# Routing, diagonals, scatters and row loads moved in a three-stage fused kernel, and one matmul group moved in each of its steps

## The chip, the cores and the metric

The kernel runs on one core of one Trainium2 chip. A core has five engines, each with an instruction queue of its own: TensorE (PE in the profile; its weight loads are PEld), VectorE (DVE), ScalarE (ACT), GpSimd (POOL) and SyncE (SP, which here only issues DMAs). They meet through semaphores. The metric is device time in microseconds (us); lower is better.

## The reference

Three layers follow each other on 3072 tokens (4 batches of 768), each of 384 values (8 heads of 48). The first is a recurrence over time, the second sends each token to one of 8 experts, the third is a dense layer.

```python
for t in range(S):                                   # 4 batches, 8 heads, 768 steps, 48 x 48 states
    cur = np.einsum('bhd,bhe->bhde', u[None] * kt, vt)
    y[:, :, t] = np.einsum('bhd,bhde->bhe', rt, state + cur)
    state = w[None, :, :, None] * state + np.einsum('bhd,bhe->bhde', kt, vt)
...
expert_idx = np.argmax(x @ w_gate, axis=1)           # one of 8 experts for each token
for e in range(E):
    xe = x[expert_idx == e]
    out[expert_idx == e] = gate_w[expert_idx == e, None] * (np.maximum(xe @ w1[e], 0.0) @ w2[e])
...
h = x @ w_in                                         # 384 -> 2048 -> 384
return (np.maximum(0.01 * h, h) @ w_out)
```

## The kernel before

**Attention: 24 units, 25 steps.** The recurrence is cut into units of one batch and 128 time steps; unit `n` is batch `n % 4`, chunk `n // 4`. The loop `for n in range(NU + 1)` in `attention` issues one step for each unit, pipelined by hand: nothing is scheduled later, every engine runs its instructions in the order of this text. In step `n`, PE does `scores(n)` (`pa`), then for unit `n-1` `values` (`py`: first the product of the state `St` with `R`, then that of `A` with `v`) and `update` (`pu`), then `rows(n-2)` (`pr`). DVE masks the scores into `A`, makes `K` and `R` two units ahead, reduces `av`, and adds `pu` to the state. ACT makes the diagonal of `A` (`prep_diag`, eight instructions), copies `py` to `xT`, decays `St`, and copies the rows out. POOL makes `rk` (two instructions) three units ahead and `kr`. `py`, `pa` and `pu` have one buffer each.

**Routing and scatter.** Four units (one chunk of all batches) are a group. `ROUTE_AT` says in which step each of the four parts of a group's routing is issued; they give the expert of each token and `ix`, its row in `xs` in DRAM. `SCATTER_AT` says in which step each unit's 128 rows are scattered there: an indirect DMA that POOL issues (`xs<-rows,ix`). Behind the scatters of groups 0 to 3, in step 21, POOL issues `load_rows(0)`: the first 256 rows of the expert that leads at half time (`choose_first`, `early_flag`). Some rows of `xs` are zeroed first (`ZERO_AT`, `xs<-z`), and a list of tokens is filled (`none`).

**Experts.** `experts` runs nine windows of rows (`WINDOWS`: two for the first expert, one for each of the others; their sizes are `CAPS`), of eight `f` each. A window's rows are loaded by `load_rows` (tile `erows`, one buffer, `w` partitions of `nj` rows each), turned by PE (`turn`, tile `pt`) into `xe`, and multiplied by PE (`first`: `ph`; `second`: `y`). An expert's weights come in eight pieces (`raw<-in_wE`, three buffers), which ACT (`piece_high`) and DVE or POOL (`piece_low`) split into two parts. All these loads but two are issued by SP, in the order of the text. Beside them the weights of the last layer are converted (`raw<-in_w2nd`, `w2f<-t`).

**The dense layer** (`second_part`, tiles `ph` and `o`) takes the rest of the time, on PE almost without a gap.

Of the kernel before, what the change touches and what calls it, by code (L numbers as in the profile page):

```python
# [36 lines left out]
WARM = 5  # L37
ZERO_AT = 3
# [4 lines left out]
    **{11 + 4 * g + u: [(g, u)] for g in (0, 1) for u in range(4)},  # L43
    19: [(2, 0), (2, 1)],
    20: [(2, 2), (2, 3)],
    21: [(3, u) for u in range(4)],
# [20 lines left out]
CAPS = (480, 456, 432, 416, 400, 392, 384, 372)  # L67
# [17 lines left out]
class Kernel:  # L85
# [150 lines left out]
    def choose_first(self, keep, part):  # L236

        V, G = self.nc.vector, self.nc.gpsimd
        if part == 0:
            f = lambda nm, w=1, dt=F32: keep.tile([1, w], dt, name=nm)  # L240
            _, self.half_key = self.counts(keep, "half", G)
            self.half_mx, self.half_x, self.half_id = f("half_mx"), f("half_x", E), f("half_id")
            self.lead, self.first_i = f("lead", E), f("first_i", 1, I32)
        elif part == 1:
            V.tensor_reduce(out=self.half_mx, in_=self.half_key, axis=AX.X, op=ALU.max)
            G.tensor_scalar(
                out=self.lead, in0=self.half_key, scalar1=self.half_mx, scalar2=None, op0=ALU.is_equal
            )
            G.tensor_tensor(out=self.half_x, in0=self.lead, in1=self.place, op=ALU.mult)
        else:  # L250
            V.tensor_reduce(out=self.half_id, in_=self.half_x, axis=AX.X, op=ALU.add)
            G.tensor_scalar(
                out=self.first_i, in0=self.half_id, scalar1=float(E - 1), scalar2=0.0, op0=ALU.min, op1=ALU.max
            )
# [10 lines left out]
    def early_flag(self, keep, part):  # L265

        V, G = self.nc.vector, self.nc.gpsimd
        if part == 0:
            self.early_cnt, _ = self.counts(keep, "early", G)
            G.tensor_tensor(out=self.early_cnt, in0=self.early_cnt, in1=self.lead, op=ALU.mult)  # L270
# [74 lines left out]
    def attention(self, xs, clist, extra, first_weights, const, route):  # L345
        nc, tc, a = self.nc, self.tc, self.a
        with ExitStack() as ctx:
# [30 lines left out]
            load(1, ("kT", "rT", "k", "r"))  # L378
# [22 lines left out]
            warm, spread = (ps.tile([P, 512], F32, tag="rt", name=nm) for nm in ("warm", "spread"))  # L401
            for i in range(WARM):
                nc.tensor.matmul(warm, self.ident, zeros, start=True, stop=True)
# [60 lines left out]
            def prep_diag(n):  # L464
# [4 lines left out]
                if n >= NU - 2:  # L469

                    flat = d["A"].rearrange("s i p t -> s p i t")
                    nc.gpsimd.tensor_tensor(
                        out=flat, in0=self.ident[:, None, None, :].to_broadcast([P, NP, 2, P]),
                        in1=d["av"].rearrange("s (p i) -> s p i", i=2)[:, :, :, None].to_broadcast([P, NP, 2, P]),
                        op=ALU.mult,
                    )
                    return
# [36 lines left out]

            def values(n):
                d, b, c = st[n], n % B, n // B
                d["py"] = py = ps1.tile([HP, NP, P], F32, tag="py", name="py")
                if c:
                    for p in range(NP):
                        nc.tensor.matmul(  # L520
                            py[:, p, :], St[b][:, p, :], d["R"][:, p, :], start=(p == 0), stop=False,
                            skip_group_check=True,
                        )
                for p in range(NP):
                    for i in range(2):
# [3 lines left out]
                            start=(c == 0 and p == 0), stop=(p == NP - 1), skip_group_check=True,  # L529
# [66 lines left out]
            for n in range(NU + 1):  # L596
# [23 lines left out]
                if 0 <= n - 1 < NU:  # L620
                    values(n - 1)
                    update(n - 1)
                if 0 <= n - 2 < NU - 1:
                    rows(n - 2)
# [15 lines left out]
                if n + 1 < NU - 2:  # L640
                    prep_diag(n + 1)
                prep_av(n + 2)
                if n + 2 >= NU - 2:
                    prep_diag(n + 2)
# [11 lines left out]
                for part, g in ROUTE_AT.get(n, ()):  # L656
# [5 lines left out]
                    self.route(part, g, route, nc.gpsimd if n < 20 else nc.vector, bank)  # L662
# [33 lines left out]
    def route(self, part, g, sm, eng, bank=None):  # L696
# [20 lines left out]
        elif part == 1:  # L717
# [139 lines left out]

    def load_rows(self, i, xs, eng=None):

        k, off, cap = WINDOWS[i]  # L860
        nj = -(-cap // P)
        w = cap // nj
# [6 lines left out]
    def turn(self, i, ps, tag, cs=range(KD)):  # L869
        nc = self.nc  # L870
        k, off, cap = WINDOWS[i]
        nj = -(-cap // P)
        w = cap // nj
# [72 lines left out]
    def experts(self, xs, clist, pools, meanwhile):  # L946
# [361 lines left out]
def main_path(k, ctx, const, out, xs, clist, debug):  # L1308
# [111 lines left out]
```

## Time and profile before

| | before |
|---|---|
| median of 3 runs | 796.58 us (795.02 to 797.38) |
| profiled execution, its own time | 795.89 us |
| its span, first to last instruction | 794.2 us |
| mean granted TensorE clock | 0.977 |
| busy: PE, DVE, ACT, POOL | 755.1, 471.9, 372.5, 198.3 us |
| POOL busy from 81.6 to 131.7 us | 43.79 us |

Busy shares are means over stages. Where two instructions of one engine overlap, a row that merges several counts the time from the first start to the last end.

### The profile page before, as it was taken

The page shows a single profiled execution, that of the slowest core. Times are in us where ns is not written, and L with a number is a line of the kernel's source. Part 1 is how long each engine was busy: PE and PEld are TensorE (multiplying, and loading weights), DVE is VectorE, ACT ScalarE, POOL GpSimd, SP SyncE. Part 2 cuts the span into 40 slices and gives each one's busy share as a digit, 9 for nine tenths or more (in the row PEclk, how much of TensorE's full clock was granted, in tenths as well). Part 3 has the DMA queues.
Part 4 walks back from the last instruction along what each step waited for, and adds up shares of the span by engine and source line. Part 5 has one row for each costly group of instructions (what it writes and reads, how often), then busy time and mean ns, then how long its engine had stood idle before and what let it go on. Part 6 is the DMA issues. An engine that isn't in the chain of part 4 may idle for free.

```text
span 794.2 us, 13196 instructions
## 1 busy us (share of the span) xinstructions
PE 755.1 (95%) x4908; PEld 694.2 (87%) x4908; DVE 471.9 (59%) x837; ACT 372.5 (47%) x785; POOL 198.3 (25%) x216
## 2 busy tenths in 40 slices
PE   6999995989999999799999999999999999999994
PEld 3889884989999999799999899999999999999993
DVE  6898885548888999699873443433333343343330
ACT  6898873355545555356443523332342243233331
POOL 6867885401222222122200110020020001002001
PEclk9999997899999999999999999999999999999997
DMA  8997965368767757757530000010010001001001
GB/s 250 264 272 225 281 223 179 121 184 257 210 193 230 232 183 232 204 162 228 147 111 21 6 35 1 1 40 0 1 40 1 1 0 40 1 1 40 1 1 44
DMA packets 52372, 92.62 MB, mean 117 GB/s; under 512 B 12788, under 2 KB 30761, under 8 KB 52297
## 3 DMA queue, kind: packets, MB, share of 16 engines
q1 hardware_dynamic: 49017, 81.47, 34.6%
q0 software_dynamic: 3280, 10.21, 3.5%
q8 instruction: 40, 0.66, 0.4%
q14 instruction: 35, 0.29, 0.1%
HBM read 73.11 MB, written 18.57 MB: 115 GB/s over the span
## 4 chain that ended last, share of the span: by engine, by line
PE 75%; DMA 9%; POOL 7%; issue 3%; DVE 2%; SPq 2%; ACT 0%; POOLq 0%; ACTq 0%
PE o L1041 25%; PE ph L1022 25%; PE ph L903 12%; PE y L928 11%; DMA r<-in_r 3%; DMA erows<-xs 3%; DMA xs<-z 2%; POOL rk L446 2%; POOL xs L759 2%; POOL rk L447 1%; PE pt L880 1%; DMA raw<-in_wE 1%; SPq L368 1%; POOL kr L451 1%; DMA xs<-rows,ix 1%
## 5 line engine op out<-in xcount | busy, mean ns | idle before, releaser
L1041 PE MATMUL o<-c,gg 128*128 128x384 f32 x1152 | 215.5, 336 | 0.0
L1022 PE MATMUL ph<-x,c 128*128 128x512 f32 x864 | 213.9, 392 | 0.0
L1041 PEld LDWEIGHTS o<-c,gg 128*128 128x128 f32 x1152 | 202.1, 188 | 8.1 <-DVE gg L1031 0.2
L1022 PEld LDWEIGHTS ph<-x,c 128*128 128x128 f32 x864 | 161.2, 188 | 28.5
L1028 DVE TENSOR_TENSOR s<-s,ph 128x512 f32<-128x512 f32 x96 | 65.9, 686 | 165.4 <-ACT s L1027 165.4
L1027 ACT ACTIVATE s<-ph 128x512 f32<-128x512 f32 x96 | 57.4, 598 | 173.9 <-PE ph L1022 162.7
L903 PE MATMUL ph<-xe,c 128*128 128x256 f32 (+8 forms) x648 | 124.8, 338 | 0.0
L928 PE MATMUL y<-hh,c 128*128 128x256 f32 (+8 forms) x648 | 122.4, 333 | 1.2 <-DVE hh L909 0.7
L802 POOL TENSOR_TENSOR c<-raw,c 128x768 fp32r<-128x768 f32 x32 | 60.2, 1880 | 223.3 <-ACT c L794 159.7
L928 PEld LDWEIGHTS y<-hh,c 128*128 128x128 f32 x648 | 110.2, 189 | 3.7 <-DVE hh L909 0.9
L903 PEld LDWEIGHTS ph<-xe,c 128*128 128x128 f32 x648 | 109.8, 192 | 1.9
L1031 DVE TENSOR_TENSOR gg<-s,gg 128x512 fp32r<-128x512 f32 x96 | 66.4, 692 | 67.0 <-ACT gg L1030 66.3
L1054 POOL DMA_INDIRECT out<-z,to x24 | 24.2, 1008 | 320.9 <-ACT z L1053 302.6
L1030 ACT ACTIVATE gg<-s 128x512 fp32r<-128x512 f32 x96 | 60.7, 632 | 81.2 <-DVE s L1028 81.2
L794 ACT ACTIVATE c<-raw 128x768 fp32r<-128x768 f32 x80 | 67.1, 840 | 6.7 <-DMA raw<-in_wE 5.9
L908 ACT ACTIVATE hh<-ph 128x256 fp32r<-128x256 f32 (+8 forms) x72 | 34.4, 478 | 68.5 <-PE ph L903 65.4
L802 DVE TENSOR_TENSOR c<-raw,c 128x768 fp32r<-128x768 f32 x48 | 46.0, 962 | 13.7 <-ACT c L794 12.0
L479 ACT ACTIVATE A<-ident,av 128x128 f32<-128x128 f32 x176 | 53.8, 396 | 0.5 <-DVE av L460 0.4
L849 DVE SCALAR_TENSOR_TENSOR t<-raw,t 128x384 f32<-128x384 uint32 x32 | 44.3, 1384 | 1.1
L909 DVE SCALAR_TENSOR_TENSOR hh<-ph,hh 128x256 fp32r<-128x256 f32 (+8 forms) x72 | 38.5, 535 | 6.1 <-ACT hh L908 5.9
L496 DVE COPY_PREDICATED A<-strict,pa 128x1024 f32<-128x1024 int32 x24 | 32.4, 1351 | 3.1 <-ACT A L479 1.2
L490 PE MATMUL pa<-R,K 48*128 48x128 f32 x384 | 28.2, 287 | 5.8 <-DVE A L496 5.8
(176 smaller groups left out, 681.1 us busy)
## 6 DMA issues: line engine op xcount, KB each, us to landing
raw<-in_wE SPq DMA_DIRECT2D x64, 384.0 KB
raw<-in_w2nd SPq DMA_DIRECT2D x32, 384.0 KB
w2f<-t SPq DMA_DIRECT2D x32, 192.0 KB
raw<-w2f SPq DMA_DIRECT2D x16, 384.0 KB
k<-in_k SPq DMA_DIRECT2D x24, 192.0 KB
r<-in_r SPq DMA_DIRECT2D x24, 192.0 KB
v<-in_v SPq DMA_DIRECT2D x24, 192.0 KB
kT<-in_kT SPq DMA_DIRECT2D x40, 96.0 KB
```

Source lines behind the costliest of these rows:

```text
L479: nc.scalar.activation(out=d["A"][:, h % 2, h // 2, :], in_=self.ident, func=AF.Copy, scale=d["av"][:, h : h + 1],)
L794: self.nc.scalar.activation(out=w[:, 0, c], in_=t, func=AF.Copy)
L802: eng.tensor_tensor(out=w[:, 1, c], in0=t, in1=w[:, 0, c].bitcast(F32), op=ALU.subtract)
L849: nc.vector.scalar_tensor_tensor(out=x, in0=low.bitcast(U32), scalar=2.0**-52, in1=x, op0=ALU.mult, op1=ALU.mult)
L903: nc.tensor.matmul(ph[:, :cap], w[:, wl, c * 512 + o : c * 512 + o + P], self.xT[i][:, xl, c, :cap], start=(c == 0 and n == 0), stop=(c == ...
L928: nc.tensor.matmul(self.y[i][m][:, :cap], w[:, wl, o : o + P], t[:, xl, :cap], start=(f == 0 and n == 0), stop=(f == FF // P - 1 and n == 2),)
L1022: nc.tensor.matmul(ph, w[:, wl, c * 512 + off : c * 512 + off + P], x2[b][:, xl, c, :], start=(c == 0 and i == 0), stop=(c == KD - 1 and i ...
L1027: nc.scalar.activation(out=s, in_=ph, func=AF.Copy, scale=0.01)
L1028: nc.vector.tensor_tensor(out=s, in0=s, in1=ph, op=ALU.max)
L1030: nc.scalar.activation(out=t[:, 0, :], in_=s, func=AF.Copy)
L1031: nc.vector.tensor_tensor(out=t[:, 1, :], in0=s, in1=t[:, 0, :].bitcast(F32), op=ALU.subtract)
L1041: nc.tensor.matmul(o[b][k][:, :DM], t[:, gl, k * P : (k + 1) * P], w[:, wl, (f % 4) * DM : (f % 4 + 1) * DM], start=(f == 0 and i == 0), s ...
```

## The change

Eight edits are made together.

1. In each step PE does the products of `A` with `v` first, then `update`, then those of the state with `R` (now `values_state`). `py` is one tile for the whole loop; the warm-up writes it once.
2. Warm-up matmuls: 3, not 5. The loads of unit 1 are issued with `k` and `r` ahead of `kT` and `rT`. Zeroing and the token list start one step earlier.
3. Scatters of groups 0 and 1 are one step earlier, those of groups 2 and 3 are spread otherwise.
4. `choose_first`, `early_flag` and the one-hot `oh` go from POOL to DVE, and so do the first two parts of group 3's routing (steps 18 and 19).
5. The diagonals of the last two units, on POOL until now, go to ACT like the others.
6. The first expert's weight pieces are split, and pieces 3 to 7 loaded, mostly one step later.
7. `CAPS` are all multiples of 16 (sum 3328, was 3332), and `nj` must divide them: 448 rows are 112 x 4 (was 456, 114 x 4), 400 are 100 x 4 (was 392, 98 x 4), 368 are 92 x 4 (was 372, 124 x 3).
8. From window 2 on, the rows of the next window are issued ahead of the weight piece on SP.

```diff
-WARM = 5
-ZERO_AT = 3
+WARM = 3
+ZERO_AT = 2
 SCATTER_AT = {
-    **{11 + 4 * g + u: [(g, u)] for g in (0, 1) for u in range(4)},
-    19: [(2, 0), (2, 1)],
-    20: [(2, 2), (2, 3)],
-    21: [(3, u) for u in range(4)],
+    **{10 + 4 * g + u: [(g, u)] for g in (0, 1) for u in range(4)},
+    18: [(2, 0)],
+    19: [(2, 1), (2, 2)],
+    20: [(2, 3), (3, 0)],
+    21: [(3, u) for u in range(1, 4)],
     24: [(4, u) for u in range(4)],
 }
...
-CAPS = (480, 456, 432, 416, 400, 392, 384, 372)
+CAPS = (480, 448, 432, 416, 400, 400, 384, 368)
...
     def choose_first(self, keep, part):
-            _, self.half_key = self.counts(keep, "half", G)
+            _, self.half_key = self.counts(keep, "half")
...
     def early_flag(self, keep, part):
-            self.early_cnt, _ = self.counts(keep, "early", G)
+            self.early_cnt, _ = self.counts(keep, "early")
...
-            load(1, ("kT", "rT", "k", "r"))
+            load(1, ("k", "r", "kT", "rT"))
...
+            self.py = ps1.tile([HP, NP, P], F32, tag="py", name="py")
             for i in range(WARM):
-                nc.tensor.matmul(warm, self.ident, zeros, start=True, stop=True)
+                x = self.py.rearrange("q p t -> q (p t)") if i == 1 else warm
+                nc.tensor.matmul(x, self.ident[:, : x.shape[0]], zeros, start=True, stop=True)
...
-                if n >= NU - 2:
-                    flat = d["A"].rearrange("s i p t -> s p i t")
-                    nc.gpsimd.tensor_tensor(
...
+            def values_state(n):
+                d, b = st[n], n % B
+                if n // B:
+                    for p in range(NP):
+                        nc.tensor.matmul(
+                            d["py"][:, p, :], St[b][:, p, :], d["R"][:, p, :], start=False, stop=(p == NP - 1),
+                            skip_group_check=True,
+                        )
...
                     values(n - 1)
                     update(n - 1)
+                    values_state(n - 1)
...
-                    self.route(part, g, route, nc.gpsimd if n < 20 else nc.vector, bank)
+                    self.route(part, g, route, nc.gpsimd if n < 18 else nc.vector, bank)
...
-            if eng is V:
-                V.tensor_tensor(out=d["oh"], in0=d["eq"], in1=be(d["m2"]), op=ALU.is_equal)
-            else:
-                eng.tensor_tensor(out=d["eq"], in0=d["eq"], in1=be(d["m2"]), op=ALU.subtract)
-                eng.tensor_scalar(out=d["oh"], in0=d["eq"], scalar1=0.0, scalar2=None, op0=ALU.is_equal)
+            V.tensor_tensor(out=d["oh"], in0=d["eq"], in1=be(d["m2"]), op=ALU.is_equal)
...
+    def window(self, i):
+        k, off, cap = WINDOWS[i]
+        nj = next(n for n in range(-(-cap // P), 5) if cap % n == 0)
+        return k, off, cap, nj, cap // nj
...
         for n, (i, f) in enumerate(seq):
+            if i > 1 and f == 0 and i + 1 < len(WINDOWS):
+                self.load_rows(i + 1, xs)
             if n + AHEAD >= nf:
                 self.piece_load(n + AHEAD)
             if n >= nf:
-                if f == 0 and i + 1 < len(WINDOWS):
+                if i == 1 and f == 0:
                     self.load_rows(i + 1, xs)
...
-        for i in {20: (0,), 21: (1,), 22: (2,), 23: (3, 4), 24: (5,)}.get(n, ()):
+        for i in {21: (0,), 22: (1,), 23: (2, 3, 4), 24: (5,)}.get(n, ()):
             k.piece_high(i)
-        for i in {21: (0,), 22: (1, 2), 23: (3, 4), 24: (5,)}.get(n, ()):
+        for i in {22: (0, 1), 23: (2, 3, 4), 24: (5,)}.get(n, ()):
             k.piece_low(i)
-        for i in {21: (3,), 22: (4, 5), 23: (6, 7)}.get(n, ()):
+        for i in {22: (3, 4), 23: (5, 6, 7)}.get(n, ()):
             k.piece_load(i)
```

POOL from the last `rk` (step 20) to the load of the first 256 rows (step 21), before (`A` is a diagonal, `early` the flag, L446 and L447 make `rk`; the line numbers of before are those of the listing):

```order
L446 TENSOR_TENSOR rk<-r,k 128x384
L447 TENSOR_TENSOR rk<-rk,u_row 128x384
L472 TENSOR_TENSOR A<-ident,av 128x4x2x128
L230 TENSOR_TENSOR early_cnt<-carry,region 1x8
L232 TENSOR_SCALAR early_key<-early_cnt 1x8
L233 TENSOR_TENSOR early_key<-early_key,rev 1x8
L270 TENSOR_TENSOR early_cnt<-early_cnt,lead 1x8
L759 DMA xs<-rows,ix 24576x386 x2
L472 TENSOR_TENSOR A<-ident,av 128x4x2x128
L759 DMA xs<-rows,ix 24576x386 x4
L864 ISA
L864 DMA erows<-xs 128x2x386
```

The same place after the change:

```order
L451 TENSOR_TENSOR rk<-r,k 128x384
L452 TENSOR_TENSOR rk<-rk,u_row 128x384
L753 DMA xs<-rows,ix 24576x386 x5
L862 ISA
L862 DMA erows<-xs 128x2x386
```

Two diagonals and the flag's four instructions are gone from between the scatters, and five scatters stand behind the last `rk`, not six.

PE in one step from step 5 on, before (`R` is the scaled query, `St` the state, `kr` the scaled key):

```order
L490 MATMUL pa<-R,K 128x128 x8
L520 MATMUL py<-R,St_140 112x128 x4
L526 MATMUL py<-A,v 48x128 x8
L511 MATMUL pu<-v,kr_2_149 48x48 x8
L565 MATMUL pr<-idwg,xT_145 128x104 x4
```

The same step after:

```order
L486 MATMUL pa<-R,K 128x128 x8
L525 MATMUL py<-A,v 48x128 x8
L507 MATMUL pu<-v,kr_2_149 48x48 x8
L515 MATMUL py<-R,St_140 112x128 x4
L564 MATMUL pr<-idwg,xT_145 128x104 x4
```

`pu` is written four matmuls (eight instructions of the profile) earlier in the step, and `py` is complete eight small matmuls later.

SP at the start of the window before the last (i = 7, f = 0), before: the two pieces issued at f = 7 and f = 0, then the rows of the last window.

```order
L781 DMA raw<-in_wE 128x768
L781 ISA
L781 DMA raw<-in_wE 128x768
L864 ISA
L864 DMA erows<-xs 124x3x386
```

After:

```order
L775 DMA raw<-in_wE 128x768
L862 ISA
L862 DMA erows<-xs 92x4x386
L775 ISA
L775 DMA raw<-in_wE 128x768
```

The rows no longer stand behind the second piece, which waits for one of the three `raw` buffers.

## Rows read from the trace of the kernel before

**Rows 1.** Page: busy time and share of each engine.
```profile
PE 755.1 (95%) x4908; PEld 694.2 (87%) x4908; DVE 471.9 (59%) x837; ACT 372.5 (47%) x785; POOL 198.3 (25%) x216
```

**Rows 2.** By stretch: from:to, length, busy of each engine, PEclk, DMA share, GB/s.
```profile
81.60:108.80 27.20, 25.40 (x333) 22.78 (x333) 22.64 (x52) 23.74 (x78) 23.76 (x36) 0.94 0.88 265
108.80:131.70 22.90, 20.52 (x232) 17.75 (x230) 18.39 (x45) 10.34 (x24) 20.03 (x21) 0.93 0.58 196
```

**Rows 3.** Chain that ended last: start us, us, what.
```profile
130.17 5.16 DMA xs<-rows,ix
...
136.06 3.42 DMA erows<-xs
...
164.75 7.23 DMA raw<-in_wE
...
322.67 14.01 DMA erows<-xs
```

**Rows 4.** POOL's groups from 81.6 to 131.7: busy, mean ns, idle before, releasers.
```profile
L759 POOL DMA_INDIRECT xs<-rows,ix x13 | 15.4, 1182 | 4.5 <-issue 3.9 <-DVE A L496 0.3 <-POOL first_i L252 0.3
L446 POOL TENSOR_TENSOR rk<-r,k 128x384 f32<-128x384 f32 x7 | 7.1, 1017 | 0.0
L447 POOL TENSOR_TENSOR rk<-rk,u_row 128x384 f32<-128x384 f32 x7 | 7.0, 1005 | 0.5
L451 POOL TENSOR_TENSOR kr<-k,Grow 128x384 f32<-128x384 f32 x5 | 5.1, 1012 | 0.2
L472 POOL TENSOR_TENSOR A<-ident,av 128x1024 f32<-128x1024 f32 x2 | 3.8, 1905 | 0.0
```

**Rows 5.** Timeline of POOL: start us, us, instruction, [idle before, releaser].
```profile
14.01 1.96 POOL L451 TENSOR_TENSOR kr<-k,Grow 128x384 f32<-128x384 f32 x2 [1.13 <-ACT Grow L206]
...
121.68 2.52 POOL L759 DMA_INDIRECT xs<-rows,ix  x1 [0.30 <-DVE A L496]
```

**Rows 6.** Timeline of PE, attention.
```profile
40.80 0.57 PE L511 MATMUL pu<-v,kr 128*48 128x48 f32 x16 [0.47 <-DVE St L556]
...
97.34 1.16 PE L490 MATMUL pa<-R,K 48*128 48x128 f32 x16
...
101.93 1.16 PE L490 MATMUL pa<-R,K 48*128 48x128 f32 x16
...
139.53 1.54 PE L880 MATMUL pt<-ident,erows 128*128 128x128 f32 x6 [7.86 <-DMA erows<-xs]
```

**Rows 7.** Timelines of ACT and DVE: a diagonal, and a one-hot on DVE.
```profile
107.92 2.44 ACT L479 ACTIVATE A<-ident,av 128x128 f32<-128x128 f32 x8
...
130.94 0.19 DVE L722 TENSOR_TENSOR oh<-eq,m 128x32 bf16<-128x32 f32 x1
```

**Rows 8.** Timelines of PE and SP, windows 1 and 6 to 8.
```profile
173.15 0.37 PE L928 MATMUL y<-hh,c 128*128 128x224 f32 x1 [0.54 <-ACT hh L908]
174.20 1.16 PE L928 MATMUL y<-hh,c 128*128 128x224 f32 x8 [0.68 <-DVE hh L909]
...
295.76 0.40 SPq L864 DMA_DIRECT2D erows<-xs  x1
...
304.76 0.49 PE L880 MATMUL pt<-ident,erows 128*128 128x128 f32 x3
...
317.67 4.77 SPq L781 DMA_DIRECT2D raw<-in_wE  x2
...
318.33 0.49 PE L880 MATMUL pt<-ident,erows 128*128 128x128 f32 x3
...
325.07 1.75 PE L903 MATMUL ph<-xe,c 128*128 128x384 f32 x9
...
329.85 1.74 PE L928 MATMUL y<-hh,c 128*128 128x384 f32 x9
336.72 0.88 PE L880 MATMUL pt<-ident,erows 124*128 124x124 f32 x3 [5.14 <-DMA erows<-xs]
337.26 3.23 PE L903 MATMUL ph<-xe,c 128*128 128x384 f32 x9
```

More of the change, by code (lines that the diff above doesn't have):

```diff
@@ L236, in choose_first @@
     def choose_first(self, keep, part):
-        V, G = self.nc.vector, self.nc.gpsimd
+        V = self.nc.vector
         if part == 0:
             f = lambda nm, w=1, dt=F32: keep.tile([1, w], dt, name=nm)
-            _, self.half_key = self.counts(keep, "half", G)
+            _, self.half_key = self.counts(keep, "half")
             self.half_mx, self.half_x, self.half_id = f("half_mx"), f("half_x", E), f("half_id")
@@ L245, in choose_first @@
             V.tensor_reduce(out=self.half_mx, in_=self.half_key, axis=AX.X, op=ALU.max)
-            G.tensor_scalar(
+            V.tensor_scalar(
                 out=self.lead, in0=self.half_key, scalar1=self.half_mx, scalar2=None, op0=ALU.is_equal
             )
-            G.tensor_tensor(out=self.half_x, in0=self.lead, in1=self.place, op=ALU.mult)
+            V.tensor_tensor(out=self.half_x, in0=self.lead, in1=self.place, op=ALU.mult)
         else:
             V.tensor_reduce(out=self.half_id, in_=self.half_x, axis=AX.X, op=ALU.add)
-            G.tensor_scalar(
+            V.tensor_scalar(
                 out=self.first_i, in0=self.half_id, scalar1=float(E - 1), scalar2=0.0, op0=ALU.min, op1=ALU.max
@@ L265, in early_flag @@
     def early_flag(self, keep, part):
-        V, G = self.nc.vector, self.nc.gpsimd
+        V = self.nc.vector
         if part == 0:
-            self.early_cnt, _ = self.counts(keep, "early", G)
-            G.tensor_tensor(out=self.early_cnt, in0=self.early_cnt, in1=self.lead, op=ALU.mult)
+            self.early_cnt, _ = self.counts(keep, "early")
+            V.tensor_tensor(out=self.early_cnt, in0=self.early_cnt, in1=self.lead, op=ALU.mult)
         else:
@@ L468, in prep_diag @@
                 d["A"] = wk.tile([P, 2, NP, P], F32, tag="A", name="A")
-                if n >= NU - 2:
-                    flat = d["A"].rearrange("s i p t -> s p i t")
-                    nc.gpsimd.tensor_tensor(
[L473 to L477, printed above, removed]
                 for h in range(H):
@@ L513, in update @@
                     )
+            def values_state(n):
[6 more added lines that the diff above has]
+                        )
             def values(n):
                 d, b, c = st[n], n % B, n // B
[L517 to L523, printed above, removed]
+                d["py"] = py = self.py
                 for p in range(NP):
@@ L528, in values @@
                             d["v"][:, (2 * p + i) * D : (2 * p + i + 1) * D], d["A"][:, i, p, :],
-                            start=(c == 0 and p == 0), stop=(p == NP - 1), skip_group_check=True,
+                            start=(p == 0), stop=(c == 0 and p == NP - 1), skip_group_check=True,
                         )
@@ L639, in attention @@
                     values_out(n - 1)
-                if n + 1 < NU - 2:
-                    prep_diag(n + 1)
+                prep_diag(n + 1)
                 prep_av(n + 2)
-                if n + 2 >= NU - 2:
-                    prep_diag(n + 2)
                 if VO <= n - 1 < NU:
@@ L855, in convert @@
             del self.conv[i]
+    def window(self, i):
+        k, off, cap = WINDOWS[i]
+        nj = next(n for n in range(-(-cap // P), 5) if cap % n == 0)
+        return k, off, cap, nj, cap // nj
     def load_rows(self, i, xs, eng=None):
-        k, off, cap = WINDOWS[i]
-        nj = -(-cap // P)
-        w = cap // nj
+        k, off, cap, nj, w = self.window(i)
         self.win[i] = t = self.rowpool.tile([P, 4, RW], F32, tag="rows", name="erows")
@@ L870, in turn @@
         nc = self.nc
-        k, off, cap = WINDOWS[i]
-        nj = -(-cap // P)
-        w = cap // nj
+        k, off, cap, nj, w = self.window(i)
         for c in cs:
```

## The prediction

> **What bounds the kernel now.** I read the page first: PE is busy 95% of the span and POOL only 25% [rows 1], so at first sight only PE's work counts. That is a mean over three stages. The windows by stretch say otherwise for the end of attention: from 81.6 to 131.7 POOL is busy 43.79 of 50.1 us, more than PE's share would suggest, since PE's own busy time there holds matmuls at a lower clock (PEclk 0.94 and 0.93) [rows 2]. The chain that ended last settles it: up to 131 us it runs along POOL, then through the landing of the last scatter (5.16 us from its issue at 130.17) and through the load of the first expert's rows (3.42 us) [rows 3]; PE stands idle 7.86 us until 139.53 for those rows [rows 6]. So in this stretch every microsecond of POOL's queue ahead of the last scatter is a microsecond of the span. Later the chain leaves PE at two more places: a weight piece that takes 7.23 us to land at 164.75, and the rows of the last window, 14.01 us from their issue at 322.67 [rows 3], for which PE waits 5.14 us [rows 8]. Everything else after 142 us is PE at work, and no edit touches its amount except by four columns.
>
> **Start-up (edits 2, 1's tile, zeroing).** Two warm-up matmuls fewer and `k`, `r` of unit 1 about 0.9 us sooner could start PE sooner. But POOL's first `kr` at 14.01 waits for ACT's `Grow`, not for a load [rows 5], and everything of step 1 hangs behind it; I take 0, bounds 1 us either way (gained if the loads decide, lost if less warm-up leaves PE at the lower clock). Zeroing one step earlier moves the same bytes; `none` still stands behind the first scatter, so SP's pause there moves a step too: 0.
>
> **POOL's queue from step 14 (edits 3, 4, 5).** The two rows of the stretch hold 57 POOL instructions and 43.79 us [rows 2]. Thirteen scatters (15.4), the `rk` pairs (7.1 and 7.0), five `kr` (5.1) and two diagonals (3.8) make 38.4 [rows 4]; the other 23 share 5.4 us, 0.235 each. After the change the diagonals and 18 of those 23 are gone (the one-hots, `half`, `lead`, `first_i`, `early`, group 3's first parts), and one scatter has moved ahead of the stretch. What is left: 12 scatters at 1.18 = 14.2, `rk` 14.1, `kr` 5.1, five small ones 1.2: 34.6 us. The idle time of the stretch is 50.1 - 43.8 = 6.3, of which 4.5 stands before scatters [rows 4]; twelve of thirteen of that is 4.15, and the other 1.8, spread over 44 instructions of which 24 stay, leaves 1.0. POOL then needs 34.6 + 5.15 = 39.75 instead of 50.1: **10.3 us less**, and with it the last scatter (at about 119.9), the load of the first rows and PE's first transpose (at about 129.2).
>
> What has to keep up? PE: one undisturbed step is 101.93 - 97.34 = 4.59 us [rows 6]; the seven steps from 97.34 take at most 32.1 at that pace and end by 129.5 even if nothing was gained before step 18 and the last steps, which have no `update`, were no shorter. DVE takes over the small ones at about 0.19 each [rows 7]; 18 of them are 3.4 us beside the 9 us by which it is idle in the same stretch (41.03 busy of 50.1 [rows 2]). ACT takes two diagonals of 2.44 [rows 7] in a stretch in which it is busy 10.34 of 22.90 [rows 2]; they hide behind that. If DVE had no room, its 3.4 us would come off the 10.3.
>
> **Weight pieces (edit 6).** Pieces 3 to 7 of the first expert are now issued one step later, while the experts start ten microseconds sooner. Until now piece 5 was split well ahead. A piece took 7.23 us to land at worst [rows 3]. The split of piece 5 now stands on ACT and DVE ahead of the copies of the turned rows: between 0 and 2 us of delay; I take 0.5, since nothing but scatters competes there. **Net of the stage: 9.8.**
>
> **Window 1.** The first `y` there waits 0.54 + 0.68 = 1.22 us [rows 8], behind ACT's wait for the piece that follows the 456 rows in the same queue. With 448 rows in 112 partitions this goes or stays: 0 to 1.22; I take 0.6.
>
> **The last window (edits 7, 8).** Its rows were issued at 322.67 because the second of the two pieces of 317.67 held SP until 322.44 (a wait for a buffer). Now they go ahead of that piece, as soon as the buffer is free: after the last transpose of the window before, 318.33 + 0.49 = 318.82 [rows 8]. That is 3.85 us sooner. How long they take is open. Slow end: as the 372 rows did, 14.01; they land at 332.83, and PE, ready at 329.85 + 1.74 = 331.59, waits 1.24 instead of 5.13: 3.9 gained. Fast end: as the 384 rows, issued at 295.76 and turned at 304.76 without a wait [rows 8], so at most 9.0; no wait at all, and the slow matmuls after the pause (3.23 against 1.75 [rows 8]) go too: 6.6. I take the slow end, nearest in size, with half of the 1.48 of the slow matmuls: **4.7**. The second piece now stands behind these rows; what it loses is not seen on PE unless ACT waits for it.
>
> Here the Trainium skill bears on the edit. The rows show that 372 rows in 124 partitions took 14.01 us, and 384 rows in 128 at most 9.0 [rows 3, 8]. The Trainium skill, DMA: Bandwidth & Descriptors, section Why a DMA increments its semaphore by 16 and not by 1, says that a DMA runs on the largest number of engines, up to 16, that divides the slowest dimension. By that rule 124 partitions got 4 engines, and so do the new 92, though 368 is a multiple of 16: the new shape doesn't speed this load, and the gain is the slow end's 3.9 to 4.7; 114 got 6 and 112 get 16, which would give all of the 1.22 in window 1. The traces agree in the one pair they show.
>
> **Columns.** Four columns fewer in 144 matmuls each; a matmul of 384 columns takes 1.75/9 = 0.194 us [rows 8], so 4 x 144 x 0.194/384 = 0.3; I take 0.2. Two windows grew by 8 columns and two shrank by 4 and 8, which cancels.
>
> **Order in the step (edit 1).** The same matmuls; `py` ends later in the step by `update` (0.57 at 40.80, its wait not counted [rows 6]), which ACT has until its next step. Cost 0; the bound is the slower rival below.
>
> **The sum.** 9.8 + 0.6 + 4.7 + 0.2 = 15.3. The profiled execution took 795.89, 0.69 under the median of the runs, within their spread: 795.89 - 15.3 = **780.6 us**.
>
> **Rivals.**
>
> *The scatters meet DVE* (0.22). One scatter took 2.52 us against a mean of 1.18, right behind a wait for DVE [rows 4, 5]. Pieces 0 and 1 are now both lowered in step 22, beside the last three scatters; if each costs 1.34 more, 4.0 us are given back, and with a late piece 5 (1 to 2 us) the time is 785 to 787. Against it: only one of thirteen was so slow. The Trainium skill, SBUF — State Buffer, section SBUF: two separate sides, gives this as a rule: GpSimd can't write the descriptors of its DMAs while VectorE holds the port pair that the two share. By that rule the price hangs on where the lowering falls, as here.
>
> *More is gained* (0.12). The last rows land as fast as the 384 did (6.6), window 1 loses its wait (1.22), and the start holds without loss (10.3 plus the 1.34 of the one slow scatter): 19.7, 776.
>
> *Only the moves outside attention pay* (0.07). If another engine or the loads hold the steps at their pace of before, PE's own pace still holds: the seven steps at 4.59 end at 129.5 instead of 131.67; some 2 of the 9.8 are left, and 780.6 + 7.6 = 788 (787 to 790).
>
> *The order of the step makes it slower* (0.05). `pu` has one buffer; PE may write it only when DVE has added the last one to the state. It already waited 0.47 once, at 40.80 [rows 6], with `update` last but one in the step. Now `update` comes ahead of the state's products, sooner by one of the five groups that share the step's 4.59 us [rows 6], an estimated 0.9. If DVE runs late in every one of the 20 steps that have it, 20 x 0.9 = 18 us are lost, and 780.6 + 18 = 799. It decides against the change from 15.3 / 20, about 0.77 us a step, on. Against it: in an undisturbed stretch DVE is through with the state by then, and a PE that waits once lets DVE catch up.
>
> *It doesn't do what it says* (0.02). POOL's time is idle time in disguise, and the rows of the last window wait for the same buffer: within 0.3% of before.
>
> **Chances and range.** The forecast, 777 to 784, has 0.52; the rivals have 0.22, 0.12, 0.07, 0.05 and 0.02. About 0.3%, 2.4 us, is what a measurement of this kernel can tell from no change. Faster by more: 0.52 + 0.22 + 0.12 + 0.07 = 0.93; the same 0.02; slower 0.05. The range runs from 773 to 790, and leaves out the slower rival, no change, and the tails.
>
> **What the new profile would show.** POOL without diagonals, its last scatter ahead of the first rows at about 120 and the load about 5.9 later; PE's first transpose of `erows` near 129, after a pause of at most 5 us; the last window's rows issued right behind the transposes of the window before, and PE's pause there near 1 us; PE's steps near 4.6 us from step 14 on, with no new wait of `pu`. It would be wrong if `pu` or `py` shows waits on DVE or ACT in each step, if the scatters stretch beyond 1.2 us, or if ACT waits for a weight piece ahead of the first `ph`.

## The result, and the profile after

The changed kernel takes **783.99 us** (median of 3 runs, 782.77 to 784.43) against 796.58 before: ratio 0.984, interval 0.981 to 0.987. That is 12.6 us less; 15.3 were forecast (780.6, range 773 to 790). The profiled execution's span is 782.3 us, 11.9 less.

First the queue that the change was to shorten. POOL's timeline after, with the columns of [rows 5]:

```profile
120.89 0.97 POOL L753 DMA_INDIRECT xs<-rows,ix  x1 [0.30 <-issue]
124.29 0.78 POOL L862 DMA_DIRECT2D erows<-xs  x1 [2.43 <-DMA xs<-rows,ix]
```

And the windows by stretch, as [rows 2] of before; POOL's is the fifth busy time, 10.55 in place of 20.03:

```profile
81.60:108.80 27.20, 23.89 (x327) 21.90 (x326) 24.27 (x55) 22.04 (x72) 23.21 (x28) 0.94 0.89 270
108.80:131.70 22.90, 21.63 (x264) 19.69 (x265) 19.55 (x56) 18.63 (x52) 10.55 (x11) 1.00 0.64 201
```

The last scatter comes at 120.89, not 130.17 [rows 3], and the load of the first rows is issued at 124.29, not 136.06: 11.8 us sooner, more than the 10.3 that were forecast. The load took 3.9 us to land, so the rows were there at 128.2. But PE, in its timeline, comes for them only at 132.35, and doesn't wait for them. The last two lines are those of before, the first `ph` and, on DVE, an operation that comes up below:

```profile
41.38 0.57 PE L507 MATMUL pu<-v,kr 128*48 128x48 f32 x16 [2.06 <-DVE St L555]
97.82 0.65 PE L507 MATMUL pu<-v,kr 128*48 128x48 f32 x16 [2.90 <-DVE St L555]
101.85 1.16 PE L486 MATMUL pa<-R,K 48*128 48x128 f32 x16
132.35 0.85 PE L876 MATMUL pt<-ident,erows 128*128 128x128 f32 x6
136.68 4.21 PE L899 MATMUL ph<-xe,c 128*128 128x256 f32 x18 [2.21 <-DVE xe L880]
```
```profile
142.43 2.85 PE L903 MATMUL ph<-xe,c 128*128 128x256 f32 x18
123.84 2.35 DVE L708 TENSOR_TENSOR df<-lg,mx 128x32 f32<-128x32 f32 x1
```

The pause of 7.86 [rows 6] is gone, and its place is taken by PE's own lateness. Step 18 starts at 101.85, where before it started at 97.34 [rows 6]. Behind the pause of 2.21 the first 18 `ph` take 4.21 us at a mean granted clock of 0.50, the lower of its two levels (1.2 GHz, not 2.4); before they took 2.85 at 0.82. PE's waits from 15 to 132 us say why (what waited for what, us in total, times, longest):

```profile
PE pu L507 <- DVE St L555: 6.7, 6, 2.9
PE pa L486 <- DVE A L492: 5.0, 4, 2.1
```

Before, `pu` waited for DVE 0.7 us in all. The longest of these waits has a neighbour on DVE and POOL; their timelines:

```profile
93.47 2.40 DVE L232 TENSOR_TENSOR half_cnt<-carry,region 1x8 f32<-1x8 f32 x1
95.91 0.16 DVE L234 TENSOR_SCALAR half_key<-half_cnt 1x8 f32<-1x8 f32 x1
96.11 0.84 DVE L235 TENSOR_TENSOR half_key<-half_key,rev 1x8 f32<-1x8 f32 x1
```
```profile
93.90 1.01 POOL L456 TENSOR_TENSOR kr<-k,Grow 128x384 f32<-128x384 f32 x1
94.86 1.00 POOL L451 TENSOR_TENSOR rk<-r,k 128x384 f32<-128x384 f32 x1
95.93 1.00 POOL L452 TENSOR_TENSOR rk<-rk,u_row 128x384 f32<-128x384 f32 x1
```

Eight numbers took 2.40 us on DVE, and the operation ends (95.87) with POOL's `rk` (95.86); the next one with two operands ends (96.95) with the second `rk` (96.93). Both are edit 4's.

In the last window the change did what was forecast, and more. SP and PE, then the second transposes of before:

```profile
312.80 0.29 SPq L862 DMA_DIRECT2D erows<-xs  x1
```
```profile
312.28 0.49 PE L876 MATMUL pt<-ident,erows 128*128 128x128 f32 x3
323.90 1.74 PE L924 MATMUL y<-hh,c 128*128 128x384 f32 x9
325.47 0.48 PE L876 MATMUL pt<-ident,erows 92*128 92x92 f32 x4
332.14 0.48 PE L876 MATMUL pt<-ident,erows 92*128 92x92 f32 x4
```
```profile
345.53 0.48 PE L880 MATMUL pt<-ident,erows 124*128 124x124 f32 x3
```

The rows are issued right behind the transposes, and no wait is left. From the last transposes of one window to the first of the next it is 325.47 - 312.28 = 13.19 us; before 336.72 - 318.33 = 18.39 [rows 8]. The next stretch, up to the second transposes, takes 332.14 - 325.47 = 6.67; before it was 8.81 (to 345.53), at a mean granted clock of 0.73, not 1.00. Together 7.3 us.

The profiled 11.9 us, by the same instructions in both traces: up to the end of the first 18 `ph` 4.4 (145.28 to 140.89); up to the first `ph` of the window of 448 rows 1.6 (181.41 to 175.45); up to the last `y` ahead of the turn nothing; the turn and what follows it 7.4; behind it 1.5 lost, of which two new waits of PE for DVE make 1.25 (`ph` 0.66 at 344.29, 0.59 at 370.20). The chain that ended last leads from the first of them back over DVE and ACT to the weight piece that now stands behind the rows: issued at 316.04, it took 9.99 us to land. So edit 8 has a small price in this trace; the wait is 0.3 in two of the variants that have it (`caps_back`, `pu_two`) and nothing that is seen in the other eight.

### The profile page after: what moved, and what is told of

It is laid out like the page before. It is cut to its first block, busy times and chain, and to the rows that moved or that the text cites. A ratio compares the mean times of both kernels' runs of the same rounds, so it can differ in the third digit from the quotient of the medians.

```text
span 782.3 us, 13224 instructions
## 1 busy us (share of the span) xinstructions
PE 747.9 (96%) x4907; PEld 689.5 (88%) x4907; DVE 477.0 (61%) x854; ACT 377.4 (48%) x801; POOL 187.4 (24%) x192
## 4 chain that ended last, share of the span: by engine, by line
PE 73%; DVE 3%; DMA 2%; issue 2%; POOL 1%; ACT 0%; POOLq 0%; ACTq 0%
PE o L1040 25%; PE ph L1021 25%; PE ph L899 10%; PE y L924 10%; DMA raw<-in_wE 1%; PE pt L876 1%; DVE c L796 1%; DVE t L830 1%; DMA erows<-xs 1%; DVE t L826 0%; DVE hh L905 0%; DVE t L840 0%; POOL xs L753 0%; POOL out L1053 0%; POOL c L796 0%
## 5 line engine op out<-in xcount | busy, mean ns | idle before, releaser
L899 PE MATMUL ph<-xe,c 128*128 128x400 f32 (+7 forms) x648 | 125.6, 340 | 2.9 <-DVE xe L880 2.9
L924 PE MATMUL y<-hh,c 128*128 128x400 f32 (+7 forms) x648 | 121.6, 332 | 0.0
L904 ACT ACTIVATE hh<-ph 128x400 fp32r<-128x400 f32 (+7 forms) x72 | 34.4, 478 | 67.6 <-PE ph L899 66.4
L475 ACT ACTIVATE A<-ident,av 128x128 f32<-128x128 f32 x192 | 58.5, 391 | 0.3 <-DVE av L465 0.2
L905 DVE SCALAR_TENSOR_TENSOR hh<-ph,hh 128x400 fp32r<-128x400 f32 (+7 forms) x72 | 38.5, 535 | 7.8 <-ACT hh L904 7.8
```

The lines of the kernel that those rows point to most:

```text
L475: nc.scalar.activation(out=d["A"][:, h % 2, h // 2, :], in_=self.ident, func=AF.Copy, scale=d["av"][:, h : h + 1],)
L899: nc.tensor.matmul(ph[:, :cap], w[:, wl, c * 512 + o : c * 512 + o + P], self.xT[i][:, xl, c, :cap], start=(c == 0 and n == 0), stop=(c == ...
L924: nc.tensor.matmul(self.y[i][m][:, :cap], w[:, wl, o : o + P], t[:, xl, :cap], start=(f == 0 and n == 0), stop=(f == FF // P - 1 and n == 2),)
```

## The experiments

All but `order_alone` are the changed kernel with the edit shown. Their ratios are to the kernel before, run with them on the same chip. There the kernel before took 794 to 802 us, and the spread of the variants is wider (780 to 791), so the times can't part what differs by less than some 2 us; the traces are read for the mechanism, each as one draw.

### Is it the order of the step, or the small operations on DVE?

`order_back`, and `order_alone` the other way round on the kernel before:

```diff
-                    values(n - 1)
-                    update(n - 1)
-                    values_state(n - 1)
+                    values_state(n - 1)
+                    values(n - 1)
+                    update(n - 1)
```

> The changed kernel with edit 1 undone: in each step the state's products, then values, then update; py stays one tile. It is compared with the kernel after the change (783.99). Theory (early update): the waits of pu for DVE's addition to the state, 6.7 us in six places after the change, come from update standing two groups sooner; here most of them go, PE ends attention near 129 instead of 132.3 (the first rows, landed at 128.2, become the bound), and the time is 780.5 to 782. Rival (late DVE): DVE is late by its new work and PE waits as long in other groups (py, the next pa); PE's end of attention and the time stay within 1 us of after, 783 to 785.

> The kernel before with edit 1 alone. Theory (early update): PE gets the new waits at pu here too, some 3 to 7 us over the 20 steps, but they lie inside the 7.86 us in which PE waited for the first rows; POOL's queue is not moved by them, so the time is that of before within 1.5 us, 795 to 798, with a shorter wait ahead of the first transpose. Rival (late DVE): no new waits at pu here, since DVE has none of the moved work; the wait for the rows stays at 7.9. Second rival: POOL's queue itself is pushed back by the slower steps, and the time is 799 or more.

`choose_pool`, and `order_choose` with both:

```diff
-            _, self.half_key = self.counts(keep, "half")
+            _, self.half_key = self.counts(keep, "half", G)
...
-            V.tensor_scalar(
+            G.tensor_scalar(
```

> The changed kernel with choose_first and early_flag back on POOL, as before (oh and the first parts of group 3 stay on DVE). Theory: the small operation on DVE that took 2.40 us at 93.47 made the longest wait of pu (2.90) and the slow matmuls behind it; without it PE ends attention 3 to 4 us sooner, POOL's load of the first rows is 1 to 2.5 us later (11 small operations), and PE's first transpose comes near 130; time 781 to 783. Rival: the wait of 2.90 comes from the order of the step; another DVE operation beside POOL's scatter takes the place of the slow one, and the time stays at 783.5 to 785.

> Both together: edit 1 undone, choose_first and early_flag on POOL. Theory: the two causes overlap, since the rows bound PE from 129 to 130.5 on: 781 to 782.5, no better than the better one of the two. If they were independent and PE alone the bound, it would be 778 to 779.

| | time, us | ratio | first `pt` at | of it wait for the rows | first `ph` at |
|---|---|---|---|---|---|
| after | 783.99 | 0.984 (0.981 to 0.987) | 132.35 | 0 | 136.68 |
| order_back | 784.36 | 0.982 (0.979 to 0.984) | 131.77 | 0 | 136.22 |
| order_alone | 797.63 | 0.999 (0.997 to 1.000) | 140.22 | 7.31 | 143.13 |
| choose_pool | 785.99 | 0.983 (0.980 to 0.987) | 135.21 | 3.80 | 138.11 |
| order_choose | 785.27 | 0.983 (0.980 to 0.987) | 133.25 | 4.62 | 136.15 |

PE's waits in `order_back`, same stretch as above:

```profile
PE pa L486 <- DVE A L492: 5.4, 4, 3.4
PE pu L507 <- DVE St L556: 2.1, 3, 1.3
```

The waits of `pu` fall from 6.7 to 2.1, as expected; the first transpose comes only 0.6 sooner, not 3, and the time, 784.36, is in the rival's range (783 to 785), though the waits of `pa` grew by no more than 0.4. `order_alone` came out as its first theory said: the new order alone brings the wait at the same place, and POOL's queue hides it:

```profile
41.50 0.56 PE L513 MATMUL pu<-v,kr 128*48 128x48 f32 x16 [2.06 <-DVE St L561]
...
140.22 1.54 PE L886 MATMUL pt<-ident,erows 128*128 128x128 f32 x6 [7.31 <-DMA erows<-xs]
```

`choose_pool` brings part of POOL's queue back, by ten operations of some 0.2 us. POOL, with one line of after ahead, and PE:

```profile
89.51 1.02 POOL L456 TENSOR_TENSOR kr<-k,Grow 128x384 f32<-128x384 f32 x1
```
```profile
91.87 1.02 POOL L456 TENSOR_TENSOR kr<-k,Grow 128x384 f32<-128x384 f32 x1
...
124.96 0.97 POOL L753 DMA_INDIRECT xs<-rows,ix  x1 [0.31 <-issue]
130.11 0.79 POOL L862 DMA_DIRECT2D erows<-xs  x1 [4.17 <-DMA xs<-rows,ix]
```
```profile
135.21 1.54 PE L876 MATMUL pt<-ident,erows 128*128 128x128 f32 x6 [3.80 <-DMA erows<-xs]
```

The load is 5.8 us later than after, where 1 to 2.5 were expected, and PE waits again. Not all of that is edit 4's: POOL was 2.36 us later (91.87 to 89.51) before the first of the ten, and the last scatter took 1.74 longer to land (4.17 + 0.97 against 2.43 + 0.97); some 1.7 us are left for the ten. `order_choose`, in which PE was ready at 128.63 (133.25 - 4.62), loses the same way. In neither of the two was a theory's time met: what one engine gains, the other gives back.

### Can the wait of `pu` be taken away?

`pu_two` gives `pu` two halves of one bank of PSUM (the memory that TensorE writes) in turn; `pu_two_w` undoes edit 6 as well.

```diff
-                pu = update_bank(n)[:HP, 0 : NP * D].rearrange("q (p d) -> q p d", p=NP)
+                o = n % 2 * NP * D
+                pu = update_bank(n)[:HP, o : o + NP * D].rearrange("q (p d) -> q p d", p=NP)
```

> The changed kernel with two halves of one PSUM bank for pu in turn, so that PE may write the next update while DVE still has to add the last one; nothing else differs (the order of edit 1 stays). Theory (pu holds PE): the waits of pu for DVE, 6.7 us in six places after the change and 2.06 at the same place in each of the three runs with the new order, shrink to under 1 us in all; PE is through attention before 129, waits for the first rows, first transpose between 128.2 and 130, first ph 3 us later; 3 to 5 us off the time of the changed kernel, ratio to before near 0.979. Rival (DVE is the pace): PE meets the same delay at the next pa, which waits for DVE's mask of A; waits there grow by 4 us or more, and the first transpose stays at 131 to 132.5.

> The same with edit 6 undone too: the pieces of the first expert split and loaded a step earlier, as before. Theory: with PE early, the split of the last pieces on ACT and DVE stands ahead of the copies of the turned rows (after the change: 2.21 us of PE's wait for xe); earlier pieces take 1 to 2 us of it away, 1 to 2 us off pu_two. Rival: the splits only move into steps 20 to 22, where ACT and DVE then hold PE or the scatters, and the time is that of pu_two or up to 3 us more.

Measured: 786.55 (0.984, 0.982 to 0.986) and 785.92 (0.985, 0.982 to 0.988); first `ph` at 140.11 and 141.19, the first transpose of `pu_two` at 136.17, later than either theory had it. The wait of `pu` is gone, and the rival's has come. PE's waits from 24 to 131 us in `pu_two`, and one of DVE's rows:

```profile
PE pa L487 <- DVE A L493: 8.5, 14, 1.4
```
```profile
63.26 0.72 DVE L557 TENSOR_TENSOR St<-St,pu 48x192 f32<-48x192 f32 x2 [0.69 <-PE pu L509]
```

The test is not clean: with both halves in one bank the program orders DVE's addition behind the *next* `update`, so DVE's mask, behind it, is later in every step, and steps settle at 4.9 us. No second bank was free. It shows that PE waits for DVE in this form too, not what a second buffer would be worth. Edit 6 undone made no difference that can be seen.

### The last window: order of issue or shape?

`rows_behind` undoes edit 8, `caps_back` edit 7.

```diff
-            if i > 1 and f == 0 and i + 1 < len(WINDOWS):
-                self.load_rows(i + 1, xs)
...
-                if i == 1 and f == 0:
+                if f == 0 and i + 1 < len(WINDOWS):
```
```diff
-CAPS = (480, 448, 432, 416, 400, 400, 384, 368)
+CAPS = (480, 456, 432, 416, 400, 392, 384, 372)
...
-        nj = next(n for n in range(-(-cap // P), 5) if cap % n == 0)
+        nj = -(-cap // P)
```

> The changed kernel with edit 8 undone: from window 2 on the next rows are issued behind the weight piece again. Theory (edit 8 makes the gain of the last window): the last window's rows are issued some 3.5 us later than after the change, and PE waits for them by 14.0 less what their new shape saves: a wait of 1 to 5 us ahead of its first transpose, followed by slow matmuls. Rival (edit 7 makes it: the new shape, 92 partitions of 4 rows, lands in 9 us or less): no wait at all, and edit 8 is worth nothing.

> The changed kernel with edit 7 undone: the sizes of before, 456 rows as 114 by 4 and 372 as 124 by 3. Theory (edit 8 makes the gain): the last rows, issued near 313, land 14.0 later, near 327, and PE, ready at 325.5, waits 1 to 1.5 us; the 456 rows bring back a wait of 0 to 1.2 us in window 1. Rival (edit 7 makes it): the 372 rows are as late as before, PE waits 3 us or more. If PE waits nowhere, the new shapes are worth only the four columns.

One run each: 789.01 and 790.79. SP and PE in `rows_behind`, then in `caps_back`:

```profile
318.95 0.28 SPq L862 DMA_DIRECT2D erows<-xs  x1
```
```profile
314.60 0.49 PE L876 MATMUL pt<-ident,erows 128*128 128x128 f32 x3
...
330.81 0.54 PE L876 MATMUL pt<-ident,erows 92*128 92x92 f32 x4 [2.85 <-DMA erows<-xs]
339.07 0.48 PE L876 MATMUL pt<-ident,erows 92*128 92x92 f32 x4
```
```profile
319.94 0.29 SPq L862 DMA_DIRECT2D erows<-xs  x1
```
```profile
319.42 0.49 PE L876 MATMUL pt<-ident,erows 128*128 128x128 f32 x3
...
332.52 0.48 PE L876 MATMUL pt<-ident,erows 124*128 124x124 f32 x3
339.15 0.48 PE L876 MATMUL pt<-ident,erows 124*128 124x124 f32 x3
```

Without edit 8 PE waits 2.85 us, and the two stretches of the turn take 16.21 + 8.26 against 13.19 + 6.67: 4.6 lost, of 7.3. Without edit 7 they take 13.10 + 6.63: nothing lost. So edit 8 without edit 7 makes the whole gain, and edit 7 without edit 8 no more than 2.7 of it. The new shape took 330.81 - 318.95 = 11.86 us to land behind the piece, the old one 14.01 before [rows 3] and at most 332.52 - 319.94 = 12.58 ahead of it: one draw each, so what the shape and the moment do to the landing is not parted. What counts is the issue, 0.5 us behind the start of the transposes and not 4.35. In `caps_back` the 456 rows bring no wait of `y` in window 1 either, so that wait was not the shape's.

Both have the attention of the changed kernel unchanged, and their first 18 `ph` end at 143.30 and 145.84, after that of after at 140.89: the spread of one and the same code there is 5 us. Much of it comes from the clock. Behind the same wait of `pu` near 42, 2.06 us, PE in after and in `choose_pool`:

```profile
41.88 1.13 PE L515 MATMUL py<-R,St 112*112 112x128 f32 x8
```
```profile
42.54 2.05 PE L515 MATMUL py<-R,St 112*112 112x128 f32 x8
```

In after the granted clock stays at 1.00, and the two steps around it (6 and 7) take 11.05 us. In the four other traces with this wait (`order_alone`, `choose_pool`, `rows_behind`, `caps_back`) its mean over them is 0.68 to 0.76, and they take 14.2 to 15.8. So the trace of after is a lucky one at this place.

### Can DVE's delays be taken away one by one?

`decay_first` has ACT decay the state ahead of the diagonal in step 5; `both` also makes the first key from PSUM and the expert from the key's low bits; `both_order` puts the old order of the step on top of it, `both_w` undoes edit 6 instead.

```diff
+                if n == B + 1:
+                    decay(n - 1)
                 prep_diag(n + 1)
...
-            _, self.half_key = self.counts(keep, "half")
+            V.scalar_tensor_tensor(
+                out=self.half_key, in0=bank[0:1, B * E : 5 * E], scalar=16.0, in1=self.key0, op0=ALU.mult, op1=ALU.add
+            )
```

> The changed kernel with one move: in step 5, the first step that decays a state, ACT decays it ahead of the diagonal, not behind it. Theory (a late DVE addition turns into a wait of pu under the new order): the 2.06 us at 41.4 to 42.5, the same in five runs with the new order, comes from DVE's addition waiting 1.81 us for that decay; here it goes, and so do the slow matmuls behind it; steps 6 to 8 take 4.4 to 4.9 each, the first transpose of the first rows comes 2 to 5 us sooner than after the change unless the wait at half_cnt returns larger; time 779 to 782, ratio to before 0.977 to 0.981. Rival (DVE or ACT is the pace): the same us turn up as a wait of pa or py in the next steps, and the first transpose stays at 131.5 or later.

> The same, and choose_first without a DVE operation that reads two operands from SBUF: the first key is the sum in PSUM times 16 plus a row that POOL made in step 13, and the expert is read from the low bits of the largest key. Theory (such operations on DVE stand still until POOL's own operation is over: 2.40 and 0.84 after the change, 2.61 for half_x in one run): none of choose_first's operations takes over 0.3 us, no wait of PE over 1 us from step 6 to 21, first transpose at 127.5 to 129 and bound by the landing of the rows, time 778 to 780.5. Rival: the operation isn't what holds DVE, and the wait at 97 stays, on another instruction.

> As the one before, with the order of the step of before (edit 1 undone). Theory: with the late additions gone the new order is the better one, since an undisturbed step takes 4.39 us with it and 4.59 without; over some 18 steps 3.6 us, of which the landing of the rows hides part; this kernel is 0 to 3 us slower than the one before it, with steps of 4.6. Rival: the old order is never worse, same time within 0.5 us or faster.

> As the second, with edit 6 undone (weight pieces a step earlier). Theory: with PE and the rows ready near 128, the split of piece 5 and the parts of the routing hold DVE's copy of the turned rows; pieces a step earlier take 0.5 to 2 us off the wait of the first ph for xe. Rival: they hold ACT and DVE in steps 20 to 22 instead, and the first ph comes no sooner or up to 2 us later.

| | time, us | ratio | first `pt` at | first `ph` at |
|---|---|---|---|---|
| decay_first | 783.66 | 0.984 (0.980 to 0.988) | 134.67 | 138.94 |
| both | 786.59 | 0.986 (0.983 to 0.990) | 132.78 | 137.30 |
| both_order | 786.19 | 0.985 (0.982 to 0.989) | 130.58 | 134.85 |
| both_w | 784.20 | 0.984 (0.981 to 0.986) | 135.18 | 139.27 |

The wait at 42 is gone in `decay_first`, as expected; the next step takes 6.18 us in place of 4.39, with waits of 0.63 for ACT and 0.88 for POOL, so that steps 6 and 7 take 10.99 us, hardly less than the 11.05 of after: it turns up again, as the rival had it. The first transpose comes 2.3 us later than in after, not 2 to 5 sooner, and 783.66 is not in the theory's range (779 to 782). The wait at `half_cnt` stays:

```profile
42.67 0.56 PE L507 MATMUL pu<-v,kr 128*48 128x48 f32 x16 [0.15 <-DVE St L555]
...
97.40 0.56 PE L507 MATMUL pu<-v,kr 128*48 128x48 f32 x16 [2.95 <-POOL pos L745]
```

(POOL's `pos` is the last event before it; the addition of DVE, held by `half_cnt` for 2.41 us, is what `pu` needs.) In `both` `half_key` takes 0.15, and the delay turns up on another of edit 4's operations. DVE, POOL, PE:

```profile
88.99 2.70 DVE L727 TENSOR_TENSOR oh<-eq,m 128x32 bf16<-128x32 f32 x1
```
```profile
89.67 1.02 POOL L459 TENSOR_TENSOR kr<-k,Grow 128x384 f32<-128x384 f32 x1
90.63 1.00 POOL L454 TENSOR_TENSOR rk<-r,k 128x384 f32<-128x384 f32 x1
```
```profile
92.56 0.81 PE L510 MATMUL pu<-v,kr 128*48 128x48 f32 x16 [1.91 <-DVE St L558]
```

In `both_order` and `both_w` it is `lead` (2.18 and 2.19 us), in `order_back` `oh` (2.23), in `rows_behind` `oh` and `half_x` (2.44, 2.61); in `choose_pool` and `order_choose`, with only `oh` and the first parts of group 3 left on DVE, none. The expectation that no wait over 1 us would be left, and 778 to 780.5, failed: not one operation is slow, but whichever of the moved ones meets POOL's pair of operations. `both_order`, expected up to 3 us slower than `both`, has its first transpose 2.2 sooner and the same time, the rival's outcome; `both_w` waits 2.15 us for `xe` where `both` waits 2.39, so 0.24 less and not 0.5 to 2, and its first `ph` comes 2.0 later, as its rival had it. None of the nine variants of the changed kernel with repeated runs is shown to beat it; they lie at 0.982 to 0.986.

## Why the prediction was right, and where it was off

**The sign, the range and POOL's queue** held: 9.3 us sooner at the last scatter and 11.8 at the load, against 10.3. Edits 3 and 5 were not undone alone; the last scatter stands at 118.8 to 126.1 in all variants with them, at 130.2 and 131.1 in the two kernels without. That this queue sets the end of attention if it is long is shown by `order_alone` and `choose_pool`, where PE waits for the rows. That the time lies in the range is in part luck: attention gave 5.4 less than its term, the turn of the last window 2.6 more and window 1 1.0 more, and the tail took back 1.5.

**The term that failed is the net of attention, 9.8.** Measured up to the end of the first 18 `ph`: 4.4 in the trace of after, 2.0 and -0.6 in the two others with the same attention (`rows_behind`, `caps_back`). In after, of the 10.3, PE's lateness took 3.1 (132.35, not 129.2), the wait for `xe` 1.4 (4.33 behind the transposes, not 2.90) and the lower clock behind it 1.4 (4.21, not 2.85); the prediction had 0.5 for all of this. The failing sentence is that the seven steps from 97.34 "end by 129.5 even if nothing was gained before step 18". They started 4.5 us later, because steps 6 to 17 now lost time. PE was the next to be late, at 131.67, so that no more than 139.53 - 131.67 = 7.86 could be had, unless PE itself came sooner. It came later by 0.7. The rival in which the steps hold PE (0.07) had this mechanism, though not the time (787 to 790).

**Edit 1 at cost 0** is not settled. The wait that the slower rival described is there (6.7 us, 2.06 of it at the same place in each of five traces with this order; `decay_first` takes that one away, and it comes back in the next step), in six steps rather than all 20. Against it stands a gain that was not foreseen: an undisturbed step takes 106.24 to 110.63, 4.39, in place of 4.59. The first `ph` came at 134.85 to 136.22 in the three traces with the old order, at 136.68 to 141.92 in the seven with the new one and one buffer. The timed runs don't bear that out: 16 of the old order (`order_back`, `order_choose`, `both_order`) have a mean of 784.2, 23 of the new one (`choose_pool`, `decay_first`, `both`, `both_w`) 785.0, with a standard error of 1.0 on the difference. What it costs over many runs stays open, between a gain of 1 and a loss of some 3 us.

**Edit 4 on DVE at 0.19 each** was the wrong price: 18 operations at 0.19 were to hide in DVE's idle time, and in all ten traces that have them there one or two of them took 1.85 to 2.70. The trace of before could have told: its `df`, of the same kind and shape as `oh`, took 2.35 us (shown above) and ended at 126.19, with POOL's diagonal of 124.22 (126.13). The Trainium skill, SBUF — State Buffer, section SBUF: two separate sides, says that VectorE and GpSimd lock a pair of ports that they share for a whole instruction, VectorE when it has two inputs from SBUF (the engines' memory on the chip) or runs in a mode that uses two ports. The rows agree: 2.40 us up to the end of POOL's `rk`, 0.15 with one operand from PSUM; in every one of the eleven places the operation ends with the `rk`, after a `kr` and that `rk`, two instructions of POOL and not one. `lead`, with one tensor and one scalar from SBUF, took 2.18; whether it ran in such a mode no run shows. The prediction used the rule for POOL's scatters alone. In after they kept to 0.97 to 1.06 us from 84 us on, and no piece was lowered beside the last ones (the first at 122.05); where one was, in `order_choose` and `both_w`, three scatters took 1.36 to 1.62, so 0.4 to 0.65 more each, not 1.34.

**Weight pieces at 0.5**: `ph` comes 4.33 us behind the first transposes, not 2.90, but 4.09 to 4.52 also in `both_w` and `both`, with and without edit 6. It is DVE's own remaining work of the last steps, piece 5 (134.11 to 135.07) and parts of the routing, that stands ahead of `xe` when PE is not held by the rows (2.90 again in `choose_pool` and `order_choose`): 1.4 us, of which edit 6 is at most 0.4. The mechanism was right, within its bounds of 0 to 2; its size was not, nor that edit 6 made it: piece 5 stands in step 24 before and after.

**The last window at 4.7** was 7.3: the whole wait with what lies around it (5.2) and the slow matmuls (2.1); the fast end (6.6) was the nearer one. The reason given, edit 8, is shown by `rows_behind` and `caps_back`, one trace each. **Window 1 at 0.6** was 1.6; both waits of `y` [rows 8] are gone in after, though `caps_back` shows that not the shape took them away. **Start-up at 0**: scores of step 2 at 21.20 after and 19.78 to 22.12 in the variants, 19.89 before; no gain, and a loss of up to 2 us not parted from the spread. **Columns at 0.2**: one window grew by 8 columns, not two, and two shrank by 8 and 4, which leaves the same four; up to the last `y` ahead of the turn nothing is seen of them, as the four are in the last window.

## What to carry to other kernels

A kernel's own trace can hold the price already: look for the longest case of an operation, not the usual one. Before a queue is shortened, read when the engine behind it would be ready: that difference, not the queue's saving, is the most that can be won, and the engine's own steps must be counted over the whole stage, not from its best stretch. Small operations are cheap only where nothing holds their engine; moved beside another engine that shares its ports they cost here what one or two of that engine's operations last, and with single buffers the delay reached PE. A load that is wanted at a fixed moment goes ahead of any transfer that may wait for a buffer.

## What the runs showed of the hardware that was not expected

- DVE operations on 8 to 32 numbers a partition took 1.85 to 2.70 us in eleven places of ten traces; in each POOL ran two tensor operations of 1.0 us back to back (`kr`, `rk`), and they lasted up to the end of the second. In before and `order_alone` one took 2.35 and 2.36, up to the end of a diagonal of 1.9 us.
- The same 32 small matmuls of a step (64 instructions of the profile) take 4.39 us with the products of the state behind `update`, and 4.59 with them ahead of those of `A`: 0.2 us by order alone; why is not shown.
- The same wait of 2.06 us of PE was followed by matmuls at the lower clock in four of five traces, and not in after. In `choose_pool` a group that takes 1.13 took 2.05; the stretch of 40 to 60 us there (busy PE, PEld, DVE, ACT, POOL, granted clock, DMA share, GB/s):

```profile
40.00:60.00 20.00, 17.95 (x196) 16.98 (x198) 13.41 (x29) 15.59 (x52) 12.63 (x21) 0.74 0.92 269
```

- The variants of the changed kernel vary more from run to run (39 runs of seven variants, standard deviation 2.9 us) than `order_alone` (12 runs, 1.0) and the kernel before (17 runs beside it, 1.7). It is not settled by whether PE waits for POOL's rows: in their traces `choose_pool` and `order_choose` do, and vary by 3.0 and 3.6; `both_w` does not, and varies by 1.0.
